# A gated recurrence by one cumulative product per chunk in place of seven halving levels, in a fused HGRN2 and mixture-of-experts kernel

## The chip, the core and the metric

The kernel runs on one core of a Trainium2 chip. The metric is the device time of one execution in microseconds; several executions are timed and their median is given. One further execution was taken with the hardware profiler; its trace gives every row below. The core has TensorE (PE; its weight loads are shown apart as PEld), VectorE (DVE), ScalarE (ACT), GpSimd (POOL) and SyncE (SP), which here only starts DMAs.

## What is computed

All inputs are float32. A recurrence with a gate per channel runs over 768 tokens, for 4 batches and 8 heads of 48 channels; its output, 3072 rows of 384, goes through a layer of 8 experts of which each row takes the one with the highest logit.

```python
f = 1.0 / (1.0 + np.exp(-f_logit))
for t in range(S):
    state = f[:, :, t, :, None] * state + np.einsum('bhd,bhe->bhde', k[:, :, t], v[:, :, t])
    y[:, :, t] = np.einsum('bhd,bhde->bhe', q[:, :, t], state)
x = y.transpose(0, 2, 1, 3).reshape(B * S, H * D)
logits = x @ w_gate
expert_idx = np.argmax(logits, axis=1)
gate_w = softmax(logits)[expert_idx]
y = gate_w * (np.maximum(x @ w1[expert_idx], 0.0) @ w2[expert_idx])
```

q, k and v are drawn with a standard deviation of 0.1; `f_logit` is 2 with a standard deviation of 0.5.

## The kernel before

The work comes in three parts: recurrence and routing, a plan, and the experts.

**Recurrence.** Each batch is cut into 6 chunks of 128 tokens, 24 chunks in all, taken two batches at a time (`steps`), with the two batches' chunks half a chunk apart (`advance`). `load` (L168) brings q, k, f and v of a chunk with tokens on partitions, one DMA each on SP; `turned` transposes q, k and f on TensorE, so that two heads lie above each other on the 128 partitions, 64 rows for each (`DP`). ScalarE copies them out of PSUM and applies the sigmoid (L194). A score of query t and key s needs the product of the gates between s and t. It is put together by halving: seven levels, block sizes 1 to 64 (`LEVELS`). At each level (from L223) TensorE multiplies the halves of all blocks (`lps`, L227), VectorE and GpSimd multiply q and k by the gates of a block (L234, L236), VectorE halves the list of block gates (L238), and a masked copy takes those scores of the product that belong to the level (`at`, L240). The pair's two heads are kept apart by zeros in `qg`. Then `y` = scores by v (L250) plus q by the state at the chunk's start (L260), the state is updated (L272 to L295), the rows are transposed for the gate's logits (L301 to L307). At the end of a batch `route` (from L309) finds each row's expert and place, and GpSimd scatters the rows, 128 at a time, into the scratch `xs` (L130).

**Plan.** Which tile belongs to which expert is worked out on one partition (L385 to L416). Eight scatters fill the end of each expert's rows with padding (`xs<-pad`).

**Experts.** 31 tiles of 128 rows: SP reads the tile's expert and row, loads rows and w1 (L428, L430); TensorE transposes the rows (L434), multiplies by w1 (`hps`, L443) and w2 (`yps`, L457; w2 was loaded during the recurrence); the result is scaled by the gate weight and scattered to the output (L130).

The order of each engine's instructions is not the code's. The framework lays a schedule by its own estimates when the program is built; the trace shows products of one chunk between those of another. On the chip each engine then takes its instructions in that order, each waiting on semaphores.

## Time and profile before

| | us |
|---|---|
| median of 3 runs | 1062.37 |
| lowest, highest | 1060.85, 1077.97 |
| span of the profiled execution, first to last instruction | 1046.0 |
| TensorE, VectorE, ScalarE, GpSimd busy in it | 822.6, 519.0, 115.9, 207.4 |

The timed runs were taken without the profiler, so the profiled execution has no time of its own beside its span; the median lies 16.4 us above that span. In the rows below, L12 is line 12 of the kernel. A group of instructions is given as line, engine, operation, output<-inputs, shape, count. A matmul of float32 operands appears as two records, a transpose as one. "Idle before" is time in which the engine waited just before such an instruction, with what ended the wait.

### The profile page before, as it was taken

The numbers are of one execution on the slowest core, as the hardware profiler recorded it, in microseconds if no ns is written. First come the engines' busy times: TensorE is split into PE (matmuls) and PEld (weight loads), VectorE is DVE, ScalarE is ACT, GpSimd is POOL, SyncE is SP. The second block draws the span as 40 slices with busy tenths as digits, with TensorE's granted clock in tenths as the row PEclk, the third lists the DMA queues.
The fourth block names the chain that finished last, engine by engine and source line by source line (L and its number), as shares of the span: only waits on it lengthen the run. The fifth ranks groups of instructions, "written<-read, shape, count | busy, mean of one in ns | idle before, by whom it ended". The sixth has DMA issues, their size and how long they took to land.

```text
span 1046.0 us, 13595 instructions
## 1 busy us (share of the span) xinstructions
PE 822.6 (79%) x5077; PEld 712.2 (68%) x5077; DVE 519.0 (50%) x1022; ACT 115.9 (11%) x205; POOL 207.4 (20%) x267
## 2 busy tenths in 40 slices
PE   5767777777776677777777777079999999999996
PEld 4667666667676666766776766067787787787775
DVE  7686777775666777667777763311111111111111
ACT  2020111111111211111111110000000000000000
POOL 2221222221214422222222213500010010010010
PEclk8797899996878799888899975579999999999999
DMA  9364112210112211111110001355445445545540
GB/s 224 129 213 150 31 31 42 41 33 17 22 31 78 71 31 39 29 25 31 31 31 8 1 0 48 110 213 205 161 154 188 181 158 191 174 155 175 190 157 1
DMA packets 129952, 99.27 MB, mean 95 GB/s; under 512 B 102734, under 2 KB 115313, under 8 KB 129888
## 3 DMA queue, kind: packets, MB, share of 16 engines
q1 hardware_dynamic: 125024, 86.58, 27.7%
q0 software_dynamic: 4032, 11.28, 3.0%
q8 instruction: 42, 0.69, 0.3%
q10 hardware_dynamic: 832, 0.54, 0.2%
q14 instruction: 22, 0.18, 0.1%
HBM read 86.90 MB, written 12.85 MB: 95 GB/s over the span
## 4 chain that ended last, share of the span: by engine, by line
issue 35%; DVE 30%; PE 28%; POOL 4%; DMA 1%; ACT 1%; SPq 0%; POOLq 0%; ACTq 0%
DVE qg L234 14%; PE lps L227 12%; DVE at L240 7%; PE y L250 5%; PE y L260 4%; DVE qg L221 3%; POOL out_dram L130 3%; DVE at L210 3%; DVE tots L238 2%; PE dp L278 2%; PE lp L306 2%; PE dps L207 1%; PE hps L443 1%; DMA w1t<-in_moe_w_dram 1%; POOL xs L130 1%
## 5 line engine op out<-in xcount | busy, mean ns | idle before, releaser
L227 PE MATMUL lps<-qg,kg 128*128 128x128 f32 x1344 | 240.7, 335 | 125.8 <-DVE qg L221 76.6
L227 PEld LDWEIGHTS lps<-qg,kg 128*128 128x128 f32 x1344 | 214.4, 239 | 147.6 <-issue 80.2
L234 DVE TENSOR_TENSOR qg<-qg,tots 64x256 f32<-64x256 f32 x288 | 161.1, 559 | 53.8 <-PE lps L227 50.0
L443 PEld LDWEIGHTS hps<-xT,w1t 128*128 128x128 f32 x1488 | 172.1, 194 | 20.9 <-DVE xT L436 11.4
L443 PE MATMUL hps<-xT,w1t 128*128 128x128 f32 x1488 | 175.2, 278 | 13.0 <-DVE xT L436 7.8
L236 POOL TENSOR_TENSOR kg<-kg,tots 128x256 f32<-128x256 f32 x140 | 110.1, 786 | 336.6 <-PE lps L227 296.6
L457 PE MATMUL yps<-w2r,hT 128*128 x496 | 165.1, 486 | 0.0
L240 DVE COPY_PREDICATED at<-mpack,lps 128x512 f32<-128x512 uint8 x168 | 148.0, 881 | 4.5
L457 PEld LDWEIGHTS yps<-w2r,hT 128*128 128x128 f32 x496 | 91.9, 190 | 57.5
L453 DVE TENSOR_SCALAR hT<-hps 128x512 f32<-128x512 f32 x31 | 21.4, 692 | 164.8 <-PE hps L443 90.1
L130 POOL DMA_INDIRECT out_dram<-ysb,xrow x31 | 30.1, 972 | 333.1 <-DVE ysb L461 307.5
L461 DVE TENSOR_SCALAR ysb<-yps,xrow 128x384 f32<-128x384 f32 x31 | 19.1, 617 | 136.2 <-PE yps L457 136.2
L250 PE MATMUL y<-vld,at 128*128 128x48 f32 x384 | 51.0, 289 | 24.6 <-DVE at L240 24.3
L250 PEld LDWEIGHTS y<-vld,at 128*128 128x128 f32 x384 | 47.9, 203 | 30.2 <-DVE at L240 30.2
L207 PE MATMUL dps<-qg,kg 128*128 128x256 f32 x192 | 50.8, 410 | 17.9 <-ACT kg L200 17.9
L451 ACT ACTIVATE hT<-hps 128x512 f32<-128x512 f32 x31 | 18.5, 597 | 356.6 <-PE hps L443 356.6
L207 PEld LDWEIGHTS dps<-qg,kg 128*128 128x128 f32 x192 | 36.7, 201 | 27.9 <-ACT kg L200 23.3
L234 DVE TENSOR_TENSOR qg<-qg,ft 64x256 f32<-64x256 f32 x48 | 32.3, 672 | 41.3 <-PE lps L227 40.5
L260 PE MATMUL y<-state,qg 128*128 128x48 f32 x320 | 48.1, 313 | 0.0
L260 PEld LDWEIGHTS y<-state,qg 128*128 128x128 f32 x320 | 46.2, 230 | 0.0
L236 POOL TENSOR_TENSOR kg<-kg,ft 128x256 f32<-128x256 f32 x24 | 23.9, 996 | 98.4 <-PE lps L227 98.4
L274 ACT COPY kn<-kp 128x512 f32<-128x512 f32 x20 | 11.7, 586 | 244.4 <-PE kp L272 244.4
(86 smaller groups left out, 567.0 us busy)
## 6 DMA issues: line engine op xcount, KB each, us to landing
w1t<-in_moe_w_dram SPq DMA_DIRECT2D x31, 1536.0 KB, 6.6
w2r<-in_moe_w_dram SPq DMA_DIRECT2D x8, 1536.0 KB, 8.7
xrow<-xs SPq DMA_DIRECT2D x31, 200.0 KB, 2.4
fld<-in_f_logit_dram SPq DMA_DIRECT2D x24, 192.0 KB, 2.7
qld<-in_q_dram SPq DMA_DIRECT2D x24, 192.0 KB, 3.2
kld<-in_k_dram SPq DMA_DIRECT2D x24, 192.0 KB, 2.8
vld<-in_v_dram SPq DMA_DIRECT2D x24, 192.0 KB, 2.7
out_dram<-ysb,xrow POOLq DMA_INDIRECT x31, 2.6
```

Of the source, the lines that this page charges most:

```text
L130: ins = nc.gpsimd.indirect_dma_start(out=dst, out_offset=bass.IndirectOffsetOnAxis(ap=idx, axis=0), in_=src, in_offset=None, bounds_check= ...
L207: nc.tensor.matmul(ps[:, j], lhsT=kg[:, hp, :], rhs=qg[:, hp], start=True, stop=True)
L210: nc.vector.copy_predicated(at[:, 4 * g : 4 * g + 4, :], _bc(mask(0), 1, 4), ps.rearrange("p j a t -> p (j a) t"),)
L221: nc.vector.tensor_tensor(qg[r, :, a, :], qg[r, :, a, :], ft[r], op=OP.mult)
L227: nc.tensor.matmul(ps[:, hp], lhsT=kg[:, hp, :], rhs=half(qg[:, hp], m, 1), start=True, stop=True)
L234: nc.vector.tensor_tensor(q1, q1, _bc(two[r, :, :, 0], 3, m), op=OP.mult)
L236: nc.gpsimd.tensor_tensor(k0, k0, _bc(two[:, :, :, 1], 3, m), op=OP.mult)
L240: nc.vector.copy_predicated(half(at, m, 1), _bc(mask(m).rearrange("p (n r) -> p n r", r=m), 1, H), ps.rearrange("p h a (n r) -> p (h a) n ...
L250: nc.tensor.matmul(y[:, h * D : h * D + D], lhsT=at[:, h, :], rhs=vt[:, h * D : h * D + D], start=h == 0, stop=c == 0, skip_group_check=True,)
L260: nc.tensor.matmul(y[:, h * D : h * D + D], lhsT=qg[:, h // 2, h % 2, :], rhs=state[:, h // 2, :], start=False, stop=True, skip_group_chec ...
L443: nc.tensor.matmul(hp[:, f, :], lhsT=w1t[:, j, o : o + 128], rhs=xT[:, j, :], start=j == 0, stop=j == KD - 1,)
L457: nc.tensor.matmul(yp, lhsT=hT[:, f, :], rhs=w2r[:, ds(er, 1), f, :], start=f == 0, stop=f == NF - 1)
```

## The change

The recurrence is rewritten; plan and experts stay but for small edits.

- Inputs are laid out on the host: q, k and f with tokens last, so that no transposes are needed to bring channels onto partitions, and v padded to 64 columns a head. `load` starts seven DMAs a chunk (two for each of f, k and q, one for each half of the partitions, and one for v).
- `prep`: z = 1 + exp(-f) is one over the gate. Four scans along the tokens (one for each pair of heads) give its running product r over the chunk, capped at 1e19. The decay is exp(-ln r). q is multiplied by the decay, k by r, both in place.
- `score`: one product per head, with 48 rows of the array, the two heads of a pair on the upper and the lower half and in different PSUM banks; a causal mask picks the scores. k is transposed for the update.
- `rows`: y is made with channels on partitions: scores by v, and q by the state; the two heads of a pair go to different halves of the output partitions.
- `update`: the state in the units of r, then multiplied by the chunk's whole decay.
- `gate`: rows are transposed back, logits come from y directly.
- The loop runs a chunk's `prep` one step ahead, its `rows` and `gate` one step behind; `route` is called for every four chunks in place of every six of one batch. w2's slices are loaded as before, one every second step.
- A check: if any running product passed 1e18 a branch computes the whole recurrence again, token by token along a scan (in the part cut below).
- Padding rows are written by eight DMAs on SP at rows read from SBUF. The token is kept as a float, and a cast per expert tile (`dst`) makes it an index.

```diff
+RMAX, RTOP = 1e18, 1e19
...
-LEVELS = [1 << i for i in range(7)]
...
-            for m in LEVELS:
...
+        NLD = 5
+        slots = {n: [ld.tile([128, HP, C], F32, name=f"{n}{i}") for i in range(NLD)] for n in "qkf"}
+        for i in range(NLD):
+            for n in "qkf":
+                nc.gpsimd.memset(slots[n][i], 30.0 if n == "f" else 0.0)
...
+        def load(n, b, c):
+            cols = slice(c * C, c * C + C)
+            for x in "fkq":
+                for a, r in halves:
+                    nc.sync.dma_start(
+                        slots[x][n % NLD][r],
+                        srcs[x][b, :, :, cols].rearrange("(p two) d s -> two d p s", two=2)[a],
+                    )
+            vt = ld.tile([128, H, DP], F32, tag="v", name="v", bufs=NLD)
+            nc.sync.dma_start(vt, v[b, cols])
+            return vt
+        def prep(n):
+            i = n % NLD
+            f, q, k = slots["f"][i], slots["q"][i], slots["k"][i]
+            z = wk.tile([128, HP, C], F32, name="z")
+            nc.scalar.activation(z, f, AF.Exp, scale=-1.0)
+            nc.gpsimd.tensor_scalar(z, z, 1.0, 1.0, op0=OP.add, op1=OP.mult)
+            r = wk.tile([128, HP, C], F32, name="r")
+            for p in range(HP):
+                nc.vector.tensor_tensor_scan(r[:, p], z[:, p], const("top"), 1.0, OP.mult, OP.min)
+            dec = wk.tile([128, HP, C], F32, name="dec", bufs=3)
+            nc.scalar.activation(dec, r, AF.Ln)
+            nc.scalar.activation(dec, dec, AF.Exp, scale=-1.0)
+            nc.gpsimd.tensor_copy(rend[:, n], r[:, :, C - 1])
+            nc.vector.tensor_tensor(q, q, dec, op=OP.mult)
+            nc.gpsimd.tensor_tensor(k, k, r, op=OP.mult)
+            return q, k, dec
+        def score(n, q, k):
+            ps = [pss.tile([128, HP, C], F32, tag=f"s{a}", name=f"s{a}") for a in range(2)]
+            for p in range(HP):
+                for a, r in halves:
+                    nc.tensor.matmul(
+                        ps[a][:, p], lhsT=k[r, p], rhs=q[r, p], start=True, stop=True
+                    )
+            kp = pst.tile([128, HP, C], F32, tag="tr", name="kp")
+            for p in range(HP):
+                nc.tensor.transpose(kp[:, p], k[:, p], ident)
+            at = scores[n % 2]
+            for a in range(2):
+                nc.vector.copy_predicated(at[:, :, a], _bc(causal, 1, HP), ps[a])
+            kn = wk.tile([128, HP, C], F32, name="kn")
+            nc.scalar.copy(kn, kp)
+            return at, kn
+        def update(c, kn, vt, dec, old):
+            dp = psm.tile([128, HP, D], F32, tag="sm", name="dp")
+            for p in range(HP):
+                for a in range(2):
+                    nc.tensor.matmul(
+                        dp[DP * a : DP * a + DP, p],
+                        lhsT=kn[:, p, DP * a : DP * a + DP],
+                        rhs=vt[:, 2 * p + a, 0:D],
+                        start=p == 0,
+                        stop=True,
+                        skip_group_check=True,
+                    )
+            new = wk.tile([128, HP, D], F32, name="state", bufs=5)
+            last = dec[:, :, C - 1 : C].to_broadcast([128, HP, D])
+            if c:
+                nc.vector.tensor_tensor(new, dp, old, op=OP.add)
+                nc.vector.tensor_tensor(new, new, last, op=OP.mult)
+            else:
+                nc.vector.tensor_tensor(new, dp, last, op=OP.mult)
+            return new
+        def rows(c, at, vt, q, old, xr):
+            yt = psy.tile([128, HP, C], F32, name="yt")
+            for p in range(HP):
+                for a in range(2):
+                    nc.tensor.matmul(
+                        yt[DP * a : DP * a + DP, p],
+                        lhsT=vt[:, 2 * p + a],
+                        rhs=at[:, p, a],
+                        start=p == 0,
+                        stop=c == 0,
+                        skip_group_check=True,
+                    )
+            if c:
+                for p in range(HP):
+                    for a, r in halves:
+                        nc.tensor.matmul(
+                            yt[r, p],
+                            lhsT=old[r, p],
+                            rhs=q[r, p],
+                            start=False,
+                            stop=True,
+                            skip_group_check=True,
+                        )
+            ys = wk.tile([128, HP, C], F32, name="ys")
+            nc.scalar.copy(ys, yt)
+            return ys
+        def gate(ys, xr, lg):
+            tp = pst.tile([128, HP, 2, DP], F32, tag="tr", name="xtp")
+            for p in range(HP):
+                nc.tensor.transpose(
+                    tp[:, p].rearrange("p a d -> p (a d)"), ys[:, p], ident
+                )
+            lp = psm.tile([128, E], F32, tag="sm", name="lp")
+            for p in range(HP):
+                nc.tensor.matmul(
+                    lp, lhsT=ys[:, p], rhs=wg[:, p], start=p == 0, stop=p == HP - 1
+                )
+            nc.scalar.copy(
+                xr[:, 0:DM].rearrange("p (h d) -> p h d", d=D),
+                tp.rearrange("p h a d -> p (h a) d")[:, :, 0:D],
+            )
+            nc.vector.tensor_copy(lg, lp)
...
+        def front(n):
+            x = chunk[n]
+            x["q"], x["k"], x["dec"] = prep(n)
+        for n in range(min(NLD - 2, NS)):
+            chunk[n]["v"] = load(n, *steps[n])
+        front(0)
+        for n in range(NS + 2):
+            if n + NLD - 2 < NS:
+                chunk[n + NLD - 2]["v"] = load(n + NLD - 2, *steps[n + NLD - 2])
+            if n % 2 == 0 and 1 <= n // 2 <= E:
+                e = n // 2 - 1
+                nc.sync.dma_start(w2r[:, e], moe_w2[e].rearrange("(f p) d -> p f d", p=128))
+            if n < NS:
+                b, c = steps[n]
+                x = chunk[n]
+                if n + 1 < NS:
+                    front(n + 1)
+                x["at"], x["kn"] = score(n, x["q"], x["k"])
+                x["old"] = per_b[b]["state"]
+            if 0 <= n - 1 < NS:
+                b, c = steps[n - 1]
+                x = chunk[n - 1]
+                x["ys"] = rows(c, x["at"], x["v"], x["q"], x["old"], None)
+            if n < NS:
+                b, c = steps[n]
+                x = chunk[n]
+                if c < NC - 1:
+                    per_b[b]["state"] = update(c, x["kn"], x["v"], x["dec"], x["old"])
+            if 0 <= n - 1 < NS:
+                m = n - 1
+                x = chunk[m]
+                g, j = m // 4, m % 4
+                if j == 0:
+                    group["xr"] = wk.tile([128, 4, ROW], F32, name="xr", bufs=3)
+                    group["lg"] = wk.tile([128, 4, E], F32, name="lg")
+                    nc.gpsimd.memset(group["xr"][:, :, USED:ROW], 0.0)
+                gate(x["ys"], group["xr"][:, j], group["lg"][:, j])
+                if j == 3:
+                    rp = psm.tile([128, 2, 4, E], F32, tag="sm", name="rp")
+                    toks = wk.tile([128, 4], F32, name="toks")
+                    for jj in range(4):
+                        bb, cc = steps[4 * g + jj]
+                        nc.gpsimd.tensor_copy(
+                            toks[:, jj : jj + 1], tok[:, bb * NC + cc : bb * NC + cc + 1]
+                        )
+                    route(
+                        wk,
+                        rp,
+                        group["lg"],
+                        [base[:, 4 * g + jj] for jj in range(5)],
+                        group["xr"],
+                        toks,
+                        "xs",
+                    )
...
+        ok = wk.tile([128, B * NC * HP], F32, name="ok", bufs=1)
+        okc = wk.tile([128, 1], F32, name="okc", bufs=1)
+        nc.vector.tensor_scalar(
+            ok, rend.rearrange("p n h -> p (n h)"), RMAX, None, op0=OP.is_le
+        )
+        nc.vector.reduce_sum(okc, ok, axis=AX_X)
+        op = psm.tile([128, 1], F32, tag="sm", name="op")
+        nc.tensor.matmul(op, lhsT=const("ones"), rhs=okc, start=True, stop=True)
+        bad = wk.tile([128, 1], F32, name="bad", bufs=1)
+        nc.vector.tensor_scalar(bad, op, float(128 * B * NC * HP) - 0.5, None, op0=OP.is_lt)
+        badi = cpool.tile([128, 1], I32, name="badi")
+        nc.vector.tensor_copy(badi, bad)
+        nc.vector.tensor_copy(end, base[:, B * NC])
+    flag = nc.values_load(badi[0:1, 0:1], min_val=0, max_val=1)
+    with tc.If(flag > 0):
...
+    endi = cpool.tile([1, E], I32, name="endi")
+    nc.vector.tensor_copy(endi, end[0:1])
+    for e in range(E):
+        row = nc.sync.value_load(endi[:, e : e + 1], min_val=e * REGION, max_val=e * REGION + N)
+        ins = nc.sync.dma_start(xs[ds(row, C)], pad).ins
+        tc.declare_no_dep(ins, group="xs", reason="no row is written twice")
+        tc.add_to_no_dep_group("xs", ins)
...
+        dst = ep.tile([128, 1], I32, name="dst", bufs=3)
+        nc.vector.tensor_copy(dst, xt[:, TOK : TOK + 1])
...
+        scatter(out, dst, ysb, N - 1, "out")
```

## Rows read from the trace of the kernel before

**Rows 1.** Stretches: PE, PEld, DVE, ACT, POOL busy (instructions); clock, DMA share, GB/s.

```profile
200.00:400.00 200.00, 146.77 (x907) 134.60 (x907) 140.26 (x292) 33.68 (x58) 54.76 (x69) 0.83 0.19 44
...
400.00:590.00 190.00, 140.62 (x935) 129.69 (x934) 137.00 (x260) 26.53 (x49) 45.87 (x59) 0.88 0.12 23
...
625.00:640.00 15.00, 10.24 (x44) 9.04 (x42) 8.72 (x29) 2.00 (x3) 3.27 (x4) 0.50 0.00 1
...
660.00:1030.00 370.00, 335.34 (x2037) 267.10 (x2038) 57.67 (x105) 17.92 (x30) 41.96 (x44) 0.96 0.49 170
```

**Rows 2.** The page's chain that ended last, shares of the span by line.

```profile
DVE qg L234 14%; PE lps L227 12%; DVE at L240 7%; PE y L250 5%; PE y L260 4%; DVE qg L221 3%; POOL out_dram L130 3%; DVE at L210 3%; DVE tots L238 2%; PE dp L278 2%; PE lp L306 2%; PE dps L207 1%; PE hps L443 1%; DMA w1t<-in_moe_w_dram 1%; POOL xs L130 1%
```

**Rows 3.** The chain in order of time: start us, us, what (records).

```profile
569.63 1.79 PE y L260 x16
...
572.35 0.94 PE lps L227 x8
...
575.14 0.57 PE lp L306 x6
...
617.50 3.56 PE y L250 x16
```

**Rows 4.** Timeline of TensorE at full clock: start us, us, what; transposes, one record each.

```profile
576.32 0.60 PE L181 MATMUL fp<-fpack,fld 128*128 128x128 f32 x4
...
576.75 0.60 PE L181 MATMUL qp<-fpack,qld 128*128 128x128 f32 x4
```

**Rows 5.** Groups by line and shape: count | busy us, mean ns | idle before them.

```profile
L393 DVE TENSOR_TENSOR_SCAN stop<-fpack,nt 1x8 f32<-1x8 f32 x1 | 0.2, 161 | 0.0
...
L238 DVE TENSOR_TENSOR tots<-tots 128x128 f32<-128x128 f32 x24 | 7.0, 292 | 0.8
...
L221 DVE TENSOR_TENSOR qg<-qg,ft 64x512 f32<-64x512 f32 x48 | 32.6, 679 | 0.7
...
L123 POOL MEMSET pad<- 128x400 f32 x1 | 0.4, 432 | 0.3 <-POOLq L475 0.3
...
L236 POOL TENSOR_TENSOR kg<-kg,tots 128x256 f32<-128x256 f32 x140 | 110.1, 786 | 336.6 <-PE lps L227 296.6 <-issue 26.3 <-DVE tots L238 6.8
...
L200 ACT COPY kg<-kp 128x512 f32<-128x512 f32 x24 | 14.1, 586 | 19.5 <-PE kp L181 17.9 <-POOL kg L236 1.5
...
L194 ACT ACT_TABLE_LOAD x3 | 3.8, 1283 | 16.2 <-PE fp L181 11.2 <-DMA mpack<-c_mpack 4.9
...
L334 ACT ACT_TABLE_LOAD x3 | 3.8, 1283 | 0.1
```

**Rows 6.** Lines 234 and 240: count, ns min/median/max, first and last start.

```profile
L234 DVE TENSOR_TENSOR qg<-qg,tots x288: 399/424/967, 19.9 to 642.9; 64x256 f32<-64x256 f32 x144
...
L240 DVE COPY_PREDICATED at<-mpack,lps x168: 684/718/1320, 18.6 to 643.3; 128x512 f32<-128x512 uint8 x168
```

**Rows 7.** Timeline of ScalarE about the end of a batch.

```profile
310.50 1.28 ACT L334 ACT_TABLE_LOAD   x1
...
319.22 1.28 ACT L194 ACT_TABLE_LOAD   x1 [5.61 <-PE fp L181]
```

**Rows 8.** The page's DMA issues: KB each, us to landing.

```profile
fld<-in_f_logit_dram SPq DMA_DIRECT2D x24, 192.0 KB, 2.7
```

**Rows 9.** Timeline of the hand-over to the experts.

```profile
654.75 0.17 DVE L307 COPY lg<-lp 128x8 f32<-128x8 f32 x1 [10.70 <-PE lp L306]
...
659.08 0.97 POOL L130 DMA_INDIRECT xs<-pad,idx  x1 [10.22 <-DVE cnt L385]
...
675.79 0.98 POOL L130 DMA_INDIRECT xs<-pad,idx  x1 [0.30 <-issue]
...
679.07 0.37 SPq L428 DMA_DIRECT2D xrow<-xs  x1
...
680.21 0.34 SPq L428 DMA_DIRECT2D xrow<-xs  x1
...
687.74 7.96 PE L443 MATMUL hps<-xT,w1t 128*128 128x128 f32 x48 [5.18 <-issue]
```

398 lines of the change are left out of this document (162 added, 236 removed).

## Prediction

> **What bounds the kernel now.** I read the profile in this order: busy time by stretch, the chain that ended last (its shares by line, then its pieces in order of time), the timeline of a chunk, the groups by line and shape, the DMA issues, the timeline of the hand-over to the experts.
>
> The table of stretches [rows 1] splits the span in two. To about 655 us the recurrence runs and TensorE and VectorE are each busy some 70 to 74% of it; from 660 us on the experts run, TensorE is busy 91% of the stretch and nothing else comes near. The chain by line [rows 2] names, for the recurrence, the factor products on VectorE, the level products on TensorE and the score evictions: work that one chunk hands from engine to engine seven times. So the recurrence is bound by a chain of hand-overs between two engines that are nearly as busy as each other. Its price is 654.7 / 24 = 27 us a chunk, where 654.7 us is the copy of the last logits [rows 9]. The experts are bound by TensorE, and the change does not touch their products.
>
> **What the change removes, and what a chunk will cost.** All seven levels go. I add up each engine's work for one chunk of the new kernel, then ask how far a chunk lies above the busiest engine.
>
> *TensorE.* At the full clock a product with 128 weight columns has the same price whether 48 or 128 columns move: 8 products in 1.79 us, 4 in 0.94 us, so 0.23 us each (an fp32 product is two records) [rows 3]. A transpose starts every 0.107 us: four lie between 576.32 and 576.75 [rows 4]; a gate product takes 0.57 / 3 = 0.19 us [rows 3]. The new chunk has 8 score products, 8 of scores by v, 8 of state by q, 8 for the state's update, 8 transposes, 4 gate products and a quarter of the route's two. If halves of the array run one after the other: 32 x 0.23 + 8 x 0.107 + 4 x 0.19 + 0.15 = 9.1 us. If the two heads of a pair run at once, the 32 cost 16 x 0.23 and the sum is 5.4 us. No row shows two half-array products together, so both ends stay. I take 6.3 us, nearer the pairs, because neighbouring products use different halves and wait for nothing from each other. In the recurrence the granted clock is 0.83 and 0.88 with TensorE 73 to 74% busy [rows 1], and new chunks ask as much of it, so I divide by 0.87: 7.2 us, with ends 6.3 and 10.5.
>
> The Trainium skill ("TensorEngine Tiling (Array Packing)", Theoretical Speedup and Key Properties) gives up to 2x for a dimension of at most 64, but also says that a change of tiling mode drains the engine; a chunk changes mode five times. By the first sentence TensorE would need 6.3 us a chunk and the sum below would end at 607 us, by the second up to 10.5 us and 727; no row of this trace decides it.
>
> *VectorE.* Four scans of 128 elements: no scan of that length is in the trace. One of 8 elements takes 161 ns [rows 5], no more than other small operations, so the lower bound is the product of 128 elements, 292 ns [rows 5], 1.2 us for four; each element needs the one before, so I bound it above by twice that, 2.3 us, and take 1.6. q by the decay: 0.68 us, the row of 512 columns [rows 5]. Two masked evictions: 0.68 us each at best, 0.72 in the median, 1.32 at worst [rows 6], take 1.6. The update is two operations of 192 columns, between 0.29 us for 128 and 0.68 for 512, 0.35 each, and the logits' copy 0.17: about 0.9 [rows 5, 9]. The route's 4.3 us, from the logits' copy at 654.75 to the first scatter at 659.08 [rows 9], are now paid once for four chunks, 1.1 us a chunk. Sum 5.9 us. The evictions and products stretch when GpSimd reads at the same time: the factor product is 399 ns at best, 967 at worst [rows 6]; if all GpSimd reading lay against VectorE, 2.4 us would come on top, 8.3.
>
> *GpSimd.* k by the growth is one product of 512 columns, twice the 786 ns of 256 [rows 5], 1.6 us. The addition of 1 is bounded below by the fill of 400 columns in 432 ns [rows 5], 0.55 us for 512, above by the two-input price, 1.6; take 0.8. One scatter a chunk at 1.28 us, since 14 of them start between 659.08 and 675.79 [rows 9], and small copies: together 4.1 us, off the path.
>
> *ScalarE.* Exp, Ln, Exp, two copies of 512 columns and one of 384, at 0.59 us for 512 [rows 5] and somewhat less for 384, give 3.4 us. Then the function tables: the trace has three loads before Sigmoid and three before Exp, 1283 ns each, copies in between have none [rows 5], and every change of function paid one. Going by that, Ln and the Exp behind it each pay one a chunk: 2.6 us, 6.0 us in all. One of the two can start before its input is there (the load at 310.50 starts as the copy before it ends, while the one at 319.22 waited 5.61 us for TensorE) [rows 7]; the second lies between Ln and Exp of one chunk and cannot.
>
> *DMA.* Per chunk 192 KB each for q, k, f and 256 KB for v, in seven issues in place of four. Landing takes 2.7 us now [rows 8]; they run three chunks ahead, 20 us and more, so they are hidden. If that cover is gone (a chunk under 6 us beside w2) TensorE waits for f.
>
> So the busiest engine has 7.2 us. Before, the busiest was at 73 to 74% [rows 1], which is a factor of 1.36 from busy to chunk; that chunk had some twenty hand-overs, the new one about eight, so I take 1.2, with ends 1.0 and 1.36. A chunk is 7.2 x 1.2 = **8.6 us**; low 6.3 x 1.0 = 6.3; high 10.5 x 1.2 = 12.6 (10.5 x 1.36 would need both worst cases at once and is left out).
>
> **The sum.** *Start:* GpSimd now fills 15 whole slots (15 x 0.55 = 8.3 us) before its first addition, so chunks run from about 10 us. *Chunks:* 24 x 8.6 = 206. *Last chunk out:* evictions 1.6, 16 products 3.7, copy, transposes, gate products, about 8. The last logits are at 224 us, where before they were at 654.7.
>
> *Hand-over to the experts,* now 654.75 to 687.74 = 33.0 us [rows 9]. The scatters behind the last route fall from 14 to 4, 10 x 1.28 = 13 us less. In their place come, all on the path: the growth check (a reduction, one product, casts, about 2 us), a branch on all engines that no row prices (0 to 5 us; take 3), and eight padding writes that SP issues one by one. SP starts the loads of successive tiles 1.1 us apart, at 679.07 and 680.21 [rows 9], with two register reads and two DMAs each, so a read and a DMA are 0.6 us: 5 us, and 3 us to land before the first rows may be read. 13 saved, 13 spent: I take 33 again, ends 25 and 45.
>
> *Experts:* 687.74 to the end, 1046.0, is 358.3 us. The added cast of the token is 0.2 us of VectorE per tile, hidden behind TensorE's 11 us a tile; without that cover 31 x 0.2 = 6 us. Rows of x are released earlier, but with TensorE busy 91% there [rows 1] nothing is gained.
>
> Span: 224 + 33 + 358 = 615 us. The profiled span, 1046.0, lies 16.4 us under the median of 1062.37; this adds on again: **632 us**.
>
> **The rivals.**
> *A: one table serves Ln and Exp, the pairs overlap fully.* For it: heads are independent, and no row has Ln. Against it: each change of function so far cost a load [rows 5]. A chunk is then at about 6.5 us, set by TensorE and VectorE: 10 + 156 + 8 + 33 + 358 + 16 = 581 us. The Trainium skill ("ScalarE: Activation LUTs", Table sets: the hidden batching unit) says that one set has both exp and ln, so that ln and then exp need one load; this trace has no such pair.
> *B: TensorE runs the halves one after another, with a clock that falls.* For it: when one chunk alone ran (625 to 640 us) the clock was granted at 0.50, the lower of the two levels [rows 1], and eight products took 3.56 us instead of 1.79 [rows 3]; new chunks also have stretches in which TensorE waits for the scan. A chunk at 12.6 us gives 10 + 302 + 8 + 33 + 358 + 16 = 727 us. Against it: at 12.6 us TensorE would be busy over 80%, more than in stretches that were granted 0.83.
> *C, slower than before: the growth check trips and the fallback computes the recurrence again.* It has 16 x 48 inner rounds, each with a DMA of 2.7 us [rows 8] and more behind it, at least 2000 us. It decides at a growth of 1e18 over one chunk. From the inputs the growth is exp of the sum of ln(1 + exp(-f)): mean 6e7, largest 1.5e9. So it does not trip. Without it, a loss needs a chunk over (1062 - 16 - 358 - 33 - 18) / 24 = 26.5 us.
>
> **How the numbers follow.** Forecast 0.58, with its own range 600 to 665 us (a chunk of 7.3 to 10); A 0.20; B 0.20; C and anything like it 0.02. The range 570 to 728 us holds the forecast, most of A and the bulk of B. Faster by over 2% (about what a measurement of this kernel can tell from no change) in all but C and some unknown stall: 0.97; within 2% 0.01; slower 0.02.
>
> **What would show it.** 48 or so table loads: ScalarE's step right; one or two: A's. A start of the second head's product within a few ns of the first, or a quarter of a microsecond later: pairs or serial. Scans over 600 ns: VectorE is the bound and a chunk nearer 10 us. A granted clock near 0.5 in the recurrence: B. An experts' stretch other than 358 us would make the prediction wrong where I see no cause.

## The result and the profile after

The changed kernel takes 696.4 us (median of 4 runs, 692.53 to 696.88) where the kernel before takes 1065.9 in the runs beside it: a ratio of 0.653, interval 0.649 to 0.656. The prediction was 632 us, range 570 to 728: faster, and inside the range, but 64 us off the forecast and outside the 600 to 665 us that it gave to the forecast itself. The profiled execution took 696.35 us, its span is 694.4. Where executions of one kernel lay over 1.5% above its fastest, the times below leave them out, and of e4, whose trace is of such an execution, only the durations of single sets are read.

The steps of the sum against the trace of after:

| step | predicted | measured | difference |
|---|---|---|---|
| start to last logits | 224 | 286.5 | +62 |
| hand-over, last logits to first `hps` | 33 | 318.2 - 286.5 = 31.7 | -1 |
| experts | 358.3 | 694.4 - 318.2 = 376.2 | +18 |
| outside the span | 16.4 | 696.35 - 694.4 = 2.0 | -14 |

A chunk is (274.2 - 18.7) / 23 = 11.1 us from the first score product (18.7 us) to the first of the last chunk (274.2), where 8.6 was forecast; that is 58 of the 62 us. Two stretches of after, one of the recurrence and one of the experts, with the columns of [rows 1]:

```profile
80.00:200.00 120.00, 96.06 (x704) 79.50 (x706) 44.72 (x135) 58.52 (x81) 28.85 (x42) 0.60 0.52 151
337.00:680.00 343.00, 322.34 (x1927) 250.04 (x1926) 54.06 (x114) 17.32 (x29) 28.37 (x29) 1.00 0.45 155
```

Between 80 and 200 us TensorE is busy 96 of 120 us, a share of 0.80 where before had 0.73 and 0.74 [rows 1], but at a granted clock of 0.60 where before had 0.83 and 0.88. The groups of one chunk's work, as [rows 5] for before:

```profile
L222 DVE TENSOR_TENSOR_SCAN r<-z,fpack 128x128 f32<-128x128 f32 x96 | 35.0, 419 | 24.9 <-POOL z L219 22.9 <-issue 1.9
...
L243 DVE COPY_PREDICATED at<-mpack,s 128x512 f32<-128x512 uint8 x48 | 33.1, 724 | 30.7 <-PE s L235 30.7
L224 ACT ACT_TABLE_LOAD x24 | 30.8, 1283 | 0.4
...
L225 ACT ACT_TABLE_LOAD x23 | 29.5, 1283 | 0.4
...
L227 DVE TENSOR_TENSOR q<-q,dec 128x512 f32<-128x512 f32 x24 | 17.5, 731 | 46.2 <-ACT dec L225 46.2
```

The four scans of a chunk cost a little less than was taken (0.42 us each, starting 0.32 apart: 1.4 us for 1.6), and Ln and the Exp behind it do load a table each, 47 loads at lines 224 and 225 in 24 chunks. Two waits of VectorE stand out: 46.2 us for the decay, ahead of `q<-q,dec`, and 30.7 us for the scores. TensorE's own timeline of two sets of 8 products (16 records each) at the higher level (2.4 GHz):

```profile
282.13 1.09 PE L274 MATMUL yt<-at,v 128*64 128x128 f32 x16
283.15 1.08 PE L285 MATMUL yt<-q,state 48*48 48x128 f32 x16
```

A set of eight at the lower level (1.2 GHz):

```profile
89.07 2.08 PE L235 MATMUL s<-q,k 48*128 48x128 f32 x16
```

From the start of one set to the start of the next, eight products of two heads take 1.02 us where before eight took 1.79 [rows 3]: 0.13 us each. At the lower level a set of eight takes 2.08. What a whole chunk asks of TensorE at the higher level is seen in a run told below, e10, which has the same sets of products; there one chunk ran from its transposes `kp` to those of the next without a wait:

```profile
74.46 0.63 PE L245 MATMUL kp<-fpack,k 128*128 128x128 f32 x4
...
77.05 0.67 PE L258 MATMUL dp<-v,kn 128*64 128x48 f32 x16
...
80.22 0.64 PE L245 MATMUL kp<-fpack,k 128*128 128x128 f32 x4
```

So a chunk is 5.76 us of TensorE at the higher level. (In the clock column a stretch reads 1.00 until the first change that is recorded; the four transposes, 0.63 to 0.66 us or 1.1, tell the level there too.)

What a slow chunk looks like, all engines in order of time:

```profile
210.70 1.95 PE L285 MATMUL yt<-q,state 48*48 48x128 f32 x16
...
212.72 0.59 ACT L294 COPY ys<-yt 128x512 f32<-128x512 f32 x1 [5.76 <-PE yt L285]
213.20 0.63 ACT L218 ACTIVATE z<-f 128x512 f32<-128x512 f32 x1
...
213.92 0.62 POOL L219 TENSOR_SCALAR z<-z 128x512 f32<-128x512 f32 x1 [2.21 <-ACT z L218]
...
214.57 1.37 DVE L222 TENSOR_TENSOR_SCAN r<-z,fpack 128x128 f32<-128x128 f32 x4 [4.65 <-POOL z L219]
215.98 0.63 ACT L224 ACTIVATE dec<-r 128x512 f32<-128x512 f32 x1 [0.85 <-DVE r L222]
...
216.17 1.26 POOL L228 TENSOR_TENSOR k<-k,r 128x512 f32<-128x512 f32 x1
216.63 1.28 ACT L225 ACT_TABLE_LOAD   x1
...
217.48 1.11 PE L240 MATMUL kp<-fpack,k 128*128 128x128 f32 x4 [4.84 <-POOL k L228]
217.92 0.63 ACT L225 ACTIVATE dec<-dec 128x512 f32<-128x512 f32 x1
...
218.59 0.69 DVE L227 TENSOR_TENSOR q<-q,dec 128x512 f32<-128x512 f32 x1 [2.64 <-ACT dec L225]
```

TensorE ends the products of state by q at 212.65. ScalarE, which starts its instructions in the order laid for it, had waited 5.76 us for them; it copies `ys`, and only then comes the first Exp of a chunk ahead (z), which in the whole trace had to wait for its input once. Behind it stand GpSimd's addition, the scans, GpSimd's product with k, and TensorE's transposes at 217.48, after 4.84 us idle. On the other branch Ln, a table load and Exp lead to q at 218.59 (Ln's own load ran while the scans did), where VectorE had waited 2.64 us with the evictions queued behind.

### The profile page after: what moved, and what is told of

Its sections match the earlier page's. It is cut to its first block, busy times and chain, and to the rows that moved or that the text cites. A ratio compares the mean times of both kernels' runs of the same rounds, so it can differ in the third digit from the quotient of the medians.

```text
span 694.4 us, 10369 instructions
## 1 busy us (share of the span) xinstructions
PE 574.7 (83%) x3895; PEld 457.8 (66%) x3895; DVE 184.4 (27%) x504; ACT 164.0 (24%) x231; POOL 116.9 (17%) x185
## 4 chain that ended last, share of the span: by engine, by line
issue 48%; POOL 4%; PE 2%; SPq 1%; DMA 1%; POOLq 0%; DVE 0%
POOL out_dram L132 4%; PE hps L536 1%; DMA xrow<-xs 1%; PE yps L550 1%; SPq L467 1%; SPq L468 0%; POOLq L132 0%; POOLq L594 0%; SPq L517 0%; SPq L516 0%; SPq L519 0%; DVE ysb L554 0%; SPq L521 0%; DVE dst L529 0%
## 5 line engine op out<-in xcount | busy, mean ns | idle before, releaser
L550 PE MATMUL yps<-w2r,hT 128*128 x496 | 171.0, 493 | 13.5 <-DVE hT L546 13.5
L132 POOL DMA_INDIRECT out_dram<-ysb,dst x31 | 30.3, 978 | 361.8 <-DVE ysb L554 326.7
L529 DVE CAST dst<-xrow 128x1 int32<-128x1 f32 x31 | 4.8, 154 | 213.5 <-DMA out_dram<-ysb,dst 193.4
L274 PE MATMUL yt<-at,v 128*64 128x128 f32 x384 | 51.2, 382 | 3.8 <-DVE at L243 3.7
L235 PE MATMUL s<-q,k 48*128 48x128 f32 x384 | 48.5, 405 | 3.0 <-DVE q L227 2.9
L235 PEld LDWEIGHTS s<-q,k 48*128 48x128 f32 x384 | 40.1, 289 | 9.1 <-DVE q L227 5.4
L274 PEld LDWEIGHTS yt<-at,v 128*64 128x64 f32 x384 | 36.4, 193 | 11.4 <-DVE at L243 6.4
L222 DVE TENSOR_TENSOR_SCAN r<-z,fpack 128x128 f32<-128x128 f32 x96 | 35.0, 419 | 24.9 <-POOL z L219 22.9
L243 DVE COPY_PREDICATED at<-mpack,s 128x512 f32<-128x512 uint8 x48 | 33.1, 724 | 30.7 <-PE s L235 30.7
L305 PEld LDWEIGHTS lp<-wg,ys 128*128 128x128 f32 x192 | 33.5, 262 | 4.2 <-issue 2.2
L285 PE MATMUL yt<-q,state 48*48 48x128 f32 x320 | 34.9, 354 | 0.0
L305 PE MATMUL lp<-wg,ys 128*128 128x8 f32 x192 | 33.8, 304 | 0.9 <-ACT ys L294 0.7
```

Of the source, the lines that this page charges most:

```text
L132: ins = nc.gpsimd.indirect_dma_start(out=dst, out_offset=bass.IndirectOffsetOnAxis(ap=idx, axis=0), in_=src, in_offset=None, bounds_check= ...
L222: nc.vector.tensor_tensor_scan(r[:, p], z[:, p], const("top"), 1.0, OP.mult, OP.min)
L235: nc.tensor.matmul(ps[a][:, p], lhsT=k[r, p], rhs=q[r, p], start=True, stop=True)
L243: nc.vector.copy_predicated(at[:, :, a], _bc(causal, 1, HP), ps[a])
L274: nc.tensor.matmul(yt[DP * a : DP * a + DP, p], lhsT=vt[:, 2 * p + a], rhs=at[:, p, a], start=p == 0, stop=c == 0, skip_group_check=True,)
L285: nc.tensor.matmul(yt[r, p], lhsT=old[r, p], rhs=q[r, p], start=False, stop=True, skip_group_check=True,)
```

## The experiments

First theory, T1: TensorE's work at the lower clock is the chunk, and what went wrong is the term 0.87 for the clock. Rival T2: a loop through ScalarE's and VectorE's queues holds the chunk, and the low clock comes from TensorE's waiting. Beside them the experts' 18 us. "Last logits" is the start of the last copy `lg<-lp`. In after the first score product comes at 18.7 us and the last logits 12 us behind the last chunk's first one; what lies between are the chunks. Where a chunk's length is given below, it is counted from the first score product to the last, by 23.

| run | us | ratio to before, interval | last logits |
|---|---|---|---|
| after | 696.4 | 0.653 [0.649, 0.656] | 286.5 |
| e1_dst | 676.9 | 0.630 [0.624, 0.636] | 285.6 |
| e2_recip | 655.7 | 0.607 [0.600, 0.614] | 244.0 |
| e3_fill | 662.9 | 0.618 [0.613, 0.623] | 254.6 |
| e4_serial | 725.2 | one run | not compared |
| e5_zahead | 664.9 | 0.625 [0.615, 0.635] | 262.2 |
| e6_notab | 674.0 | 0.635 [0.622, 0.647] | 264.3 |
| e7_zfill | 671.8 | 0.636 [0.628, 0.644] | 254.4 |
| e8_all | 640.4, 645.2 | two runs | 255.1 |
| e9_less | 692.2 | 0.651 [0.646, 0.657] | 280.9 |
| e10_znotab | 614.8 | 0.580 [0.574, 0.585] | 204.3 |
| e11_best | 658.0 | 0.617 [0.612, 0.621] | 267.1 |
| e12_sig | 647.9 | 0.607 [0.602, 0.613] | 257.5 |

(The runs were made in groups, on several chips; the kernel before, run beside each group, took 1059.5 to 1070.4 us in the median. A difference of a per cent between two rows says nothing. In e6 and e10 the decay is a constant and in e9 a product is missing, so the tokens go to other experts, and only the time up to the last logits is read.)

**The experts: a buffer.**

```diff
-        dst = ep.tile([128, 1], I32, name="dst", bufs=3)
+        dst = ep.tile([128, 1], I32, name="dst", bufs=8)
```

> Eight buffers instead of three for dst, the index tile of the output scatter; nothing else. In the trace of after VectorE's cast into dst waits for the scatter of three tiles back, 193.4 us over 28 tiles, and the eviction of the second half of the hidden layer stands behind it on VectorE. Theory (the wait for the buffer is what stretched the experts from 358 to 376 us): the wait goes, the tiles fall from 12.1 to 11.5 us, the kernel is 14 to 20 us shorter, 676 to 682 us. Rival (the tiles are held by the loads of rows and weights, or by the later start of the weights, and the cast waits in time that nobody needs): less than 4 us.

Measured: 19.5 us less; first `hps` at 317.3, end at 674.3, so the experts take 357.0 us, as predicted for them. The groups of the products by w2 and of the cast in after:

```profile
L550 PE MATMUL yps<-w2r,hT 128*128 x496 | 171.0, 493 | 13.5 <-DVE hT L546 13.5
...
L529 DVE CAST dst<-xrow 128x1 int32<-128x1 f32 x31 | 4.8, 154 | 213.5 <-DMA out_dram<-ysb,dst 193.4 <-DMA xrow<-xs 20.1
```

The same two groups of e1_dst:

```profile
L550 PE MATMUL yps<-w2r,hT 128*128 x496 | 165.1, 486 | 0.0
...
L529 DVE CAST dst<-xrow 128x1 int32<-128x1 f32 x31 | 4.8, 154 | 77.4 <-DMA xrow<-xs 77.4
```

193.4 us of waiting for the output's scatter are gone, and TensorE's 13.5 us for `hT` with them. Shown: the cast cost nothing by its 0.15 us; it cost 19 us (376.2 to 357.0) by the buffer that it waited for, with the eviction of `hT` queued behind it.

**The decay without ScalarE.**

```diff
-            nc.scalar.activation(dec, r, AF.Ln)
-            nc.scalar.activation(dec, dec, AF.Exp, scale=-1.0)
+            nc.vector.reciprocal(dec, r)
```

> The decay is a reciprocal on VectorE in place of Ln and Exp on ScalarE, so no table loads are left in the chunks. Theory T1 (a chunk's 11.1 us is TensorE's work at the lower of its two clock levels): ScalarE is not the limit, TensorE's products cost the same, the last logits stay within 15 us of 286, TensorE's granted clock stays near 0.6 between 80 and 240 us; the kernel within 2% of 696 us. Rival T2 (the way from scan to decay, two activations of 0.6 us and a table load of 1.28 us between them, holds the chunk, TensorE waits for it, and the clock falls because it waits): 1.3 to 2.6 us a chunk or more are gone, 30 to 60 us, and the clock is higher. Between them: the reciprocal of 512 columns has no row yet; if it takes over 2 us, VectorE becomes the limit and the chunk grows.

The group of the reciprocal in this run, and behind it the stretch from 80 to 200 us with the columns of [rows 1]:

```profile
L224 DVE RECIPROCAL dec<-r 128x512 f32<-128x512 f32 x24 | 80.1, 3338 | 0.0
```

The stretch:

```profile
80.00:200.00 120.00, 110.48 (x996) 92.67 (x995) 95.99 (x199) 28.89 (x55) 39.32 (x55) 0.74 0.62 176
```

42 us less up to the last logits, although the reciprocal takes 3.34 us and VectorE is now busy 96 of 120 us. T2's direction; the gain stops at (229.3 - 18.3) / 23 = 9.2 us a chunk.

**Extra work for TensorE.**

```diff
+            for p in range(HP):
+                for a, r in halves:
+                    nc.tensor.matmul(ps[a][:, p], lhsT=ident, rhs=ident, start=True, stop=True)
```

> Eight extra products of 128 rows by 128 columns, constant by constant, ahead of the score products of every chunk, into the same tiles, which the score products then overwrite; all results stay. At the full clock they are 8 x 0.23 = 1.8 us of TensorE, at the half clock 3.7 us. Theory T1a (the chip grants the lower clock when the array is used by halves and with gaps, and TensorE's work at that clock is the chunk): with whole-array work in the gaps the clock is granted at 1.0 in more of the recurrence, and a chunk takes 5.5 + 1.8 = 7.3 to 8.5 us instead of 11.1; the kernel is 60 to 85 us shorter, 610 to 635 us. Rival T1b (the clock does not follow what TensorE does here): a chunk takes 11.1 + 2 to 3.7 us, the kernel 745 to 780 us. Rival T2 (another engine's chain holds the chunk and TensorE has room): no change, within 10 us, TensorE busier.

The same stretch of this run:

```profile
80.00:200.00 120.00, 108.68 (x1102) 95.93 (x1104) 55.30 (x171) 66.57 (x95) 35.61 (x50) 0.86 0.61 176
```

Adding eight products a chunk made the kernel 33 us shorter: the granted clock between 80 and 200 us rose from 0.60 to 0.86. The clock does follow what TensorE does here, and the low clock is part of the chunk, with every load still in it; so T2's "no change" is wrong. But a chunk came to (246.4 - 18.7) / 23 = 9.9 us, not T1a's 7.3 to 8.5, and the gain is half of what T1a asked for.

**Pairs.** In all four sets:

```diff
-            for p in range(HP):
-                for a, r in halves:
+            for a, r in halves:
+                for p in range(HP):
```

> The loops over the pair and over its two heads change places in all four sets of half-array products, so that neighbours use the same half of the array and the two heads no longer alternate. Theory (neighbouring products on different halves run at once): a set of eight takes 8 x 0.23 = 1.8 us at the full clock instead of 1.0, 3.6 instead of 2.1 at the half clock; 32 products cost 3.7 us more a chunk at the full clock. If the clock then is granted at 1.0 because TensorE has fewer gaps, a chunk takes about 9.2 us, and the kernel is even faster than after, 650 us; if it stays at 0.6, a chunk takes 15 us or more and the kernel 790 us. Rival (pairs run one after another in both orders): no change.

Two sets at the full clock, from this run's timeline of TensorE:

```profile
216.57 1.58 PE L274 MATMUL yt<-at,v 128*64 128x128 f32 x16
218.09 1.55 PE L285 MATMUL yt<-q,state 48*48 48x128 f32 x16
```

The same sets took 1.09 and 1.08 us in after. 0.5 us a set, under 2 us a chunk at the full clock, not the 3.7 expected: from start to start 0.19 us a product with one half against 0.13 with two. Alternating halves is worth a third of a product, and by the one time in the table the kernel is 29 us longer without it.

**ScalarE's order.** z gets three buffers, its Exp is issued two chunks ahead, and

```diff
-            nc.scalar.copy(ys, yt)
+            with tc.issue_after(zs[min(n_ + 2, NS) - 1][1]):
+                nc.scalar.copy(ys, yt)
```

> Only the order on ScalarE changes: the first Exp of a chunk (z) is issued one chunk earlier, with three buffers in place of two, and is tied ahead of the copy of the result tile ys in ScalarE's queue. In the trace of after that Exp stands behind ys, which waits for TensorE's last products: around 212.7 us TensorE ends its products, then ys 0.59, Exp 0.63, GpSimd 0.62, scans 1.37, GpSimd's product 1.26, and only then the transposes at 217.48, TensorE idle for 4.84 us; 27.8 us of such waits between 80 and 270 us. Theory T3 (this loop through ScalarE's queue leaves TensorE idle, and the clock falls behind the idle stretches): the waits of the transposes for k shrink to a few us, more of the recurrence runs at the full clock, a chunk takes 8 to 9.5 us, the last logits come at 215 to 245 us, the kernel at 625 to 660 us. Rival T1 (TensorE's work at the lower clock is the chunk, the waits are filled from elsewhere): within 15 us of 696.

TensorE's longest wait between 80 and 270 us (us in total, times, longest) in after:

```profile
PE kp L240 <- POOL k L228: 27.8, 9, 5.5
```

The same view of this run:

```profile
PE s L240 <- issue: 17.5, 8, 2.7
```

And its group of q's product on VectorE:

```profile
L232 DVE TENSOR_TENSOR q<-q,dec 128x512 f32<-128x512 f32 x24 | 16.6, 690 | 51.7 <-ACT dec L230 51.7
```

The transposes' wait is gone and 24 us with it, but a chunk is still (247.6 - 19.6) / 23 = 9.9 us, and the clock is 0.63 between 80 and 200 us: half of T3. VectorE's wait for the decay is the longest now, 51.7 us. The expectation says that only ScalarE's order changes; the two traces show that the framework laid TensorE's and VectorE's order anew as well, so that the 24 us are not the price of ScalarE's order alone.

**The table loads.**

```diff
-            nc.scalar.activation(dec, r, AF.Ln)
+            nc.scalar.activation(dec, r, AF.Exp, scale=0.0)
```

> Ln is replaced by an Exp of the same shape (of zero times the growth), so the 47 function table loads of the recurrence go and every instruction of ScalarE and of the other engines keeps its place; the decay is then a constant and the output is not the reference's. Theory T2 (the way from scan to decay on ScalarE, of which two loads are 2.57 us a chunk, is on the loop that sets the chunk): 1.3 to 2.6 us a chunk, the last logits at 227 to 256 us. Rival (ScalarE is half idle and the loads fall into its waits): last logits within 8 us of 286. Routing depends on the values, so that only the recurrence up to the last logits is to be compared.

22 us less, of the 60 that 47 loads take, between the two expectations. All four engines keep the order of after here, so this is the price of the loads there: as long as z stands behind `ys`, most of a load falls into time that is waited for anyway.

**Both of these together: ScalarE's order and the extra products.**

> Both edits at once: the first Exp one chunk earlier and ahead of ys in ScalarE's queue, and the eight extra whole-array products ahead of each chunk's score products. Alone, the first brought the last logits from 286.5 to 262.2 us with TensorE still busy 26 to 29 of every 32 us at a granted clock of 0.55 to 0.77; the second brought them to 254.6 at 0.8 to 1.0. Theory T1+T3 (two things hold a chunk, idle stretches behind ScalarE's queue and TensorE's own work at the lower clock): the gains add up to a good part, the clock is granted near 1.0 through most of the recurrence, a chunk takes 7.5 to 8.5 us, the last logits come at 200 to 225 us, the kernel at 600 to 635 us. Rival (the two edits remove the same idle time, the extra products only filled the waits): last logits at 250 us or later, and the extra products cost what they take.

The stretch from 80 to 200 us:

```profile
80.00:200.00 120.00, 108.18 (x1078) 96.05 (x1080) 58.48 (x176) 65.75 (x94) 36.52 (x53) 0.85 0.60 171
```

254.4, as with the extra products alone: the rival holds. The clock is 0.85, TensorE busy 108 of 120 us with the extra products among it, and nothing was added to the gain.

**And the product of q later, and `dst`.** q's product is tied behind the two evictions of the chunk before (`with tc.issue_after(ev)`).

> As the run with both edits, and two more: the product of q by the decay stands on VectorE behind the two score evictions of the chunk before, where it stood ahead of them and waited for the decay (45 us in after, 52 us with the earlier Exp), and dst has eight buffers. Theory: dst gives the 20 us that it gave alone; the later product of q frees VectorE's queue for the evictions and gives 0 to 1.5 us a chunk more, up to 30 us; the kernel at 560 to 610 us. Rival (TensorE's order waits for q instead of VectorE's for the decay): the 20 us of dst alone against the run with both edits.

The group of q's product in this run:

```profile
L357 DVE TENSOR_TENSOR q<-q,dec 128x512 f32<-128x512 f32 x23 | 16.8, 731 | 21.6 <-ACT dec L230 21.6
```

VectorE's wait for the decay halved against e5, and the last logits stayed at 255, as the rival said: with the extra products in, this wait isn't what ends last. The 20 us of `dst` came again.

**Less work for TensorE.** The loop over the products of state by q is left out.

> The eight products of state by q are left out of every chunk, so the output is not the reference's and the tokens go to other experts; only the recurrence up to the last logits is to be compared. They are 8 of 32 half-array products, 34.9 us of TensorE in the profile of after, 1.0 us a chunk at the full clock and 1.95 us at the half clock. Theory T1 (TensorE's work at the granted clock is the chunk): the chunk falls by 1.5 to 2 us, the last logits come 30 to 45 us earlier, at 240 to 257 us, with TensorE still busy over 80%. Rival (the loop through the other engines sets the chunk, and TensorE's clock only fills the room it leaves): the last logits come less than 15 us earlier, and either TensorE's busy share or its granted clock falls by the work that was taken away.

The stretch from 80 to 200 us, and then the longest wait of TensorE from 80 to 270 us:

```profile
80.00:200.00 120.00, 88.07 (x612) 73.54 (x609) 46.16 (x142) 59.97 (x83) 28.75 (x42) 0.56 0.51 149
```

The wait:

```profile
PE kp L240 <- POOL k L228: 42.4, 16, 5.9
```

5.6 us less, where T1 wanted 30 to 45. The work that was taken away came back as waiting: 42.4 us for GpSimd's k instead of 27.8, and a clock of 0.56. T1 as it stands, for the whole recurrence, falls. (The framework lays the order anew when work goes, so this run says that TensorE's work alone isn't the chunk, not how long the loop would be.)

**Both loads and the order.** The edit of e6 on the kernel of e5; TensorE's order is that of e5 to the instruction.

> The run with the earlier Exp (last logits at 262.2 us), with Ln replaced by an Exp of the same shape, so that the 47 table loads go while TensorE's order stays the same to the instruction; the decay is a constant and the output is not the reference's; only the recurrence is to be compared. VectorE waited there 51.7 us for the decay, 2.1 us a chunk. Theory (the loop through ScalarE and VectorE sets the chunk, whatever clock TensorE is granted): 1.3 to 2.6 us a chunk go, last logits at 200 to 232 us. Rival T1 (TensorE at the lower clock sets it): last logits within 8 us of 262.

The stretch from 80 to 200 us:

```profile
80.00:200.00 120.00, 103.44 (x1108) 88.41 (x1107) 71.23 (x220) 47.61 (x91) 44.72 (x61) 0.84 0.59 165
```

The group of q's product on VectorE:

```profile
L232 DVE TENSOR_TENSOR q<-q,dec 128x512 f32<-128x512 f32 x24 | 17.3, 719 | 13.8 <-ACT dec L230 13.8
```

204.3 against 262.2 in e5: 58 us. A chunk is (193.5 - 19.3) / 23 = 7.6 us, 2.3 less for 2.57 us of loads, and the granted clock goes from 0.63 to 0.84 with the same work in the same order, on TensorE and on the other three engines. So the loads cost these 58 us, and the low clock of e5 comes from them.

How they do it is seen in e5. From the end of a chunk's last scan to the end of its product of q are 4.8 us there on average, and 2.9 in e10. One chunk of e5, with TensorE at the higher level up to the last line:

```profile
171.87 0.41 DVE L227 TENSOR_TENSOR_SCAN r<-z,fpack 128x128 f32<-128x128 f32 x1
...
172.71 1.28 ACT L229 ACT_TABLE_LOAD   x1
...
174.00 0.63 ACT L229 ACTIVATE dec<-r 128x512 f32<-128x512 f32 x1
...
174.65 1.28 ACT L230 ACT_TABLE_LOAD   x1
...
175.94 0.63 ACT L230 ACTIVATE dec<-dec 128x512 f32<-128x512 f32 x1
...
176.60 0.69 DVE L232 TENSOR_TENSOR q<-q,dec 128x512 f32<-128x512 f32 x1 [3.68 <-ACT dec L230]
...
177.40 1.71 PE L240 MATMUL s<-q,k 48*128 48x128 f32 x16 [2.70 <-issue]
```

Here both loads lie between scan and q. The profile names no releaser for TensorE's wait of 2.70 us ("issue"), but q's product ends at 177.29, and each of the ten waits of over 0.5 us ahead of score products in e5 ends 0.1 us after that chunk's q. At the lower level TensorE hardly waits:

```profile
117.00:167.00 50.00, 46.61 (x324) 40.63 (x324) 21.55 (x64) 28.02 (x39) 14.22 (x21) 0.50 0.60 166
```

Summed over the stretches of each level from 30 to 245 us of e5, TensorE is busy 62.4 of 86.5 us at the higher level and 123.6 of 128.5 at the lower; in e10, from 30 to 190 us with nearly the same work, 100.1 of 122.6 and 37.4 of 37.4. So both theories have a part. At the higher level the way from scan over Ln, load and Exp to q holds the chunk (T2); at the lower level TensorE's own work does (T1), and there the loads cost time by bringing the lower level about. Of the 55 us between these two sums 48 are TensorE's busy time: most of the gain came by way of the clock.

**Two tries at a faster kernel.** First the reciprocal, q's product on GpSimd, and `dst`:

> Three edits meant to beat after: the reciprocal on VectorE (in the run with it alone, last logits at 244.0 us and the kernel at 656.4 us, VectorE busy 88 to 92% of the recurrence), the product of q by the decay on GpSimd, which has room there, and dst with eight buffers. dst gives its 20 us again, 636 us; if VectorE sets the chunk now, taking 0.7 us a chunk from it gives up to 16 us more, 620 us; if GpSimd's product takes 1.3 us on the way to the scores and that way sets the chunk, nothing or a loss of up to 14 us, 636 to 650 us.

TensorE's longest wait between 80 and 270 us:

```profile
PE s L234 <- POOL q L226: 15.5, 8, 2.8
```

No gain over the reciprocal alone, and worse than both expectations: `dst` gave its 20 us, and the last logits came 23 us later; TensorE now waits for GpSimd's q. Then the decay as a second scan, over Sigmoid of f:

```diff
-            nc.scalar.activation(dec, r, AF.Ln)
-            nc.scalar.activation(dec, dec, AF.Exp, scale=-1.0)
+            for p in range(HP):
+                nc.vector.tensor_tensor_scan(dec[:, p], dec[:, p], const("top"), 1.0, OP.mult, OP.min)
```

> The decay is a second scan on VectorE, over Sigmoid of f, in place of Ln and Exp of the growth. Exp and Sigmoid both read f alone, are issued for two chunks together two chunks ahead and are tied ahead of the copies of ys in ScalarE's queue; one load of each function's table serves two chunks, and dst has eight buffers. Theory (the loop that sets a chunk runs through VectorE's queue to ScalarE, its table loads and back; TensorE's clock follows): nothing on ScalarE stands between the scan and the product of q any more; the chunk, 7.6 us in the run without table loads, gets the second scan's 1.4 us on VectorE at worst, 7.6 to 9.0 us; the last logits at 204 to 240 us, TensorE's granted clock at 0.75 or more, the kernel at 590 to 630 us with the 20 us of dst. Rival (the second scan makes VectorE the bound as the reciprocal did, with a chunk of 9.2 us): last logits at 244 us or later, the kernel at 636 us or more.

The stretch from 80 to 200 us:

```profile
80.00:200.00 120.00, 89.28 (x842) 75.83 (x840) 73.67 (x216) 45.70 (x70) 34.31 (x53) 0.71 0.58 166
```

The groups of q's product on VectorE and of the route's first product on TensorE:

```profile
L238 DVE TENSOR_TENSOR q<-q,dec 128x512 f32<-128x512 f32 x24 | 16.2, 677 | 0.4
...
L157 PE MATMUL rp<-oh,fpack 128*128 128x32 f32 x12 | 3.6, 391 | 25.7 <-DVE oh L156 25.7
```

A miss: VectorE waits for no decay any more, and the last logits come at 257.5 all the same. That is the rival's number, but VectorE is not full, 74 of 120 us. In the new order the route's product `rp` stands on TensorE ahead of work that is ready and waits 25.7 us for VectorE's one-hot rows, up to 6.3 us at a time. With `dst`, this kernel is 0.93 of after (647.9 to 696.4), and e8 is like it.

## Why the prediction was right, and where it was wrong

The direction and the range held although the sum has one large error, one middling one, and one that took part of them back by luck: +62, +18, -14. The range held by its width: 696 is past the forecast's own 665, in the part that was kept for rival B.

*TensorE's sum: right, at its low end.* 5.4 us was the lower bound for pairs, 5.76 is what the rows show; 6.3 was taken. The rule of the Trainium skill ("TensorEngine Tiling (Array Packing)", Theoretical Speedup) allows up to 2x; against before's 0.23 us [rows 3] it is 1.8, against the same products one half at a time 1.5. The Trainium skill ("TensorEngine Tiling (Array Packing)", Key Properties) says that a change of tiling mode drains TensorE. The trace agrees that a change costs something, and shows that it is little: in the chunk of e10 above, the first record of a set of another mode starts 0.20 to 0.23 us after the start of the one before, where sets of one mode follow at 0.11. By an estimate from these starts five changes are some 0.5 us of the 5.76; the sum had no term for them, and the state's update took 0.67 us in place of 0.9.

*The clock, 0.87: wrong, 0.60.* This is the term in which most of the 62 us appear: TensorE is busy 0.80 x 11.1 = 8.9 us of a chunk where 7.2 was forecast, and 8.9 x 1.25 is 11.1, so that even the factor 1.2 looks right. But the clock isn't a first cause. With the loads out and e5's order of z, e10 was granted 0.84, and its chunk is 7.6 us: near the forecast's 0.87, and under its 8.6. Nor is it only a mark of waits: e3 raised it with all loads in place and gained 33 us.

*The factor 1.2 from the busiest engine to the chunk: the step that failed.* It was argued from the number of hand-overs, eight for twenty. The prediction had the pieces, "the second lies between Ln and Exp of one chunk and cannot" start early, but put the loads into ScalarE's busy time alone, 6.0 us, under TensorE's 7.2, and so at nothing. One hand-over with a load in it costs more than several without: scan 1.4, Ln 0.63, load 1.28, Exp 0.63, q 0.7, and it is paid in a loop because of the order laid, `ys` ahead of the next z on ScalarE and q ahead of the evictions on VectorE. The two loads cost 22 us in after's order (e6) and 58 in e5's (e10, there for the most part by way of the clock). No engine has to be full for that: ScalarE is busy 58.5 of 120 us.

*ScalarE, two loads a chunk: right,* 47 of 48. The rule that ln and then exp need one load ("ScalarE: Activation LUTs" of the Trainium skill, Table sets: the hidden batching unit) did not hold for the kernel as it was built; by e10 it would have been worth up to 58 us, once z is out of the way, and 22 without that (e6). Rival A's 581 us had one load and the experts at 358: e10's 614.8 less the 20 us of `dst` would be 595.

*VectorE, 5.9 us: too high,* 44.7 busy us in 120 are 4.1 a chunk; GpSimd, 4.1, is 2.7. *Start:* the fills end at 8.2 us as summed.

*Hand-over: right in sum,* 31.7 for 33. The timeline of after, rows that answer [rows 9]:

```profile
286.46 0.17 DVE L312 COPY lg<-lp 128x8 f32<-128x8 f32 x1 [4.05 <-PE lp L305]
...
295.81 0.98 POOL L132 DMA_INDIRECT xs<-xr,posi  x1 [0.30 <-issue]
...
296.47 8.35 SPq L468 DMA_DIRECT2D xs<-pad  x8
...
307.47 0.37 SPq L519 DMA_DIRECT2D xrow<-xs  x1
...
318.16 4.10 PE L536 MATMUL hps<-xT,w1t 128*128 128x128 f32 x22 [5.75 <-issue]
```

The padding writes take 8.35 us of SP, 2.6 more pass to the first load of rows, and 10.7 to the first product. The scatters, which the sum had on the path, are not on it: the last one still runs when the padding writes start. The 10 us from the last logits to these writes go by the check, whose flag SP reads at 291.2, and by the branch: SP is through it at 293.1 and reads its first row number at 295.6. So the branch, taken at 3 us without a row, cost 4.4; for 2.5 of them the profile names no cause.

*The added cast "hidden behind TensorE's 11 us": wrong.* Its own 0.15 us is hidden; the step asked what the cast costs and not what it waits for. Three buffers, and a scatter that lets go of them late, made it a wait in VectorE's queue: 19 us (e1).

*The 16.4 us outside: wrong, 2.0.* The profiled execution of before was simply a quick one: in the runs of before beside the experiments, time less span is 1.8 us (1063.47 to 1061.7). An error of 14 us that hid as much of the others.

*Rival B*, at 727 us nearer to the measured time than the forecast, had the low clock (12.6 us a chunk) and for its reason "stretches in which TensorE waits"; its serial halves were wrong. *Rival C* did not come; no growth check tripped.

*What stays open.* How much of a chunk in after each link carries: single cures gave 24 (order), 22 (loads), 32 (extra products) and 42 us (reciprocal), the pair of the first two 82, the first and third together 32. Most edits let the framework lay another order; only after against e1 and e6, and e5 against e10, are compared with the order held, and no run holds the clock while the way to q changes. Why e9's shorter set of products did not shorten the way to `ys` was not settled either.

## What to carry over

Before dividing work by engine, write down the loop that one step of a recurrence runs through, with every function table load and every instruction that stands ahead of it in its engine's queue; an engine at half load can set the time. A low granted clock beside a busy TensorE may come from waits elsewhere: ask what happens to the time when work is taken from TensorE (here 5.6 us of 286 went), and look at the stretches of each clock level separately, before calling TensorE the bound of the whole. And of an added instruction ask what it waits for, its buffer included, not only how long it takes.

## What the runs showed of the hardware

- Adding eight whole-array products a chunk raised the granted clock of the stretch from 0.60 to 0.86 and shortened the kernel by 33 us (e3).
- Half-array products of one half in a row take 0.19 us each (e4), of alternating halves 0.13 (after), whole-array ones of before 0.23 [rows 3], all at 2.4 GHz with 128 moving columns. With 48 moving columns a set of eight alternating ones takes 0.67 us in place of 1.09 (e10), where whole-array ones of 48 columns were no cheaper [rows 3].
- A change of tiling mode on TensorE at 2.4 GHz puts the next record 0.20 to 0.23 us behind the start of the one before, in place of 0.11 (e10).
- A reciprocal of 512 columns on VectorE takes 3.34 us, five times the product of the same shape in that run (0.68 us, e2).
- A load of a function table takes 1.28 us, and the two of a chunk, with ScalarE half idle, cost 58 us of the recurrence (e10 against e5).
- A scan of 128 columns takes 0.42 us, and four follow each other at 0.32 us (after).
